# Attention by pairs of heads: full-float32 scores on two row tiles, blocks of 128 queries, and a list-scheduled instruction order

## The chip, the cores and the metric

The kernel runs on one NeuronCore of one Trainium2 chip. The metric is the device time of one execution in microseconds (us), the median of three runs. Times inside an execution come from the hardware profiler and count from its first instruction.

## The reference

Causal attention over 24 heads (2 batches of 12, 448 positions, head size 64) feeds a gated layer and then a mixture of eight experts with one expert per token. Only the attention part is touched by the change.

```python
batch, n_heads, seq, head_dim = (2, 12, 448, 64)

scores = scale * np.matmul(q, k.transpose(0, 1, 3, 2))
scores = np.where(mask, -1000000000.0, scores)          # mask: upper triangle, k=1
scores = scores - np.max(scores, axis=-1, keepdims=True)
attn = np.exp(scores)
attn = attn / (np.sum(attn, axis=-1, keepdims=True) + 1e-09)
return np.matmul(attn, v).astype(np.float32)
...
x = attn_out.transpose(0, 2, 1, 3).reshape(B * S, H * D)     # 896 x 768
gate = 1 / (1 + np.exp(-(x @ w_gate)));  x = gate * (x @ w_val) @ w_out
out = gate_w[:, None] * (np.maximum(x @ w1[e], 0) @ w2[e])   # e: the token's expert
```

## The kernel before

Everything runs in one program whose instruction order on each engine is the order in which the Python code issues it; no engine reorders its own queue. PE does the matmuls, DVE the row maxima and part of the evictions, ACT the exponentials and the other evictions, POOL the normalisation, and the SP queue starts the loads.

**Attention.** Heads go in 24 steps `t`, two to a pair `p`. Queries are cut into four blocks of 112, so that block `c` needs 112(c+1) keys. Per head:

- `at_qk` (L194 for the first head of a pair, L190 and L191 for the second) makes the scores `sc`. The first head is taken as float32 from 64 partitions; the second is split into high and low parts (`at_hi` on DVE, L172; `at_lo` on POOL, L178 and L179), and is two passes over 128 partitions. `sc` lies in four PSUM banks "A".
- `at_max` (L202, DVE) adds the mask, writes the rows to `pr` and takes the row maximum; `at_exp` (L208, ACT) takes the exponential and the row sum; `at_recip` (L213, L214, DVE) and `at_norm` (L220, POOL, four blocks) normalise.
- `at_T` (L232) transposes the ten 112 x 112 blocks of `pr` into two banks "B" (`tp`); `at_ev` (L242 on ACT, L244 on DVE) copies them to `pt`.
- `at_av` (L252) multiplies by `v`, both heads of a pair in the two column halves of one bank `av`; `at_xh` (ACT) and `at_xl` (DVE) split the result into `xh` and `xl`, the operands of the next stage.

**What sets the order.** Two strings of operation names, `ORDER`, one for even and one for odd `t`, written by hand. A head's scores, its maxima, its normalisation, its transposes and its `av` are issued in different steps (`t`, `t-1`, `t-2`, `t-4`, and `(t-6)//2` for the pair).

**Weights.** The gate and value weights arrive as 64-bit numbers in pieces of 128 x 768 (`raw_gv`, through SP). `conv64` turns a piece into float32 in five DVE steps (L97 to L105), then ACT writes the high part (`whi`, L107) and POOL the low part (`wlo`, L108). The first three pieces are converted during attention: the name "w" in `ORDER` takes one DVE step, from `t` = 6 on.

```python
V.scalar_tensor_tensor(t, u[:, :, 0], 29, t, ALU.logical_shift_right, ALU.bitwise_or)
v = t.bitcast(F32)
A.copy(hi, v)
G.tensor_tensor(lo, v, hi.bitcast(F32), ALU.subtract)
```

The last two lines are issued together with the fifth DVE step. Each of the three pieces feeds one `gv` unit of batch 0 (18 matmuls, L273), issued between the last heads. After attention comes the loop over all 24 `gv` units, beginning with unit 0 of batch 1; the rest of the program (the output layer, routing, the experts) isn't touched.

Of the kernel before, what the change touches and what calls it, by code (L numbers as in the profile page):

```python
# [24 lines left out]
CP = 112  # L25
# [10 lines left out]
C_MASK = 0  # L36
C_ID = C_MASK + S
# [10 lines left out]
def _consts():  # L48
    c = np.zeros((128, C_END), np.float32)
    p = np.arange(128)[:, None]  # L50
    c[:, C_MASK + S - CP:C_MASK + S] = np.where(np.arange(CP)[None, :] > p, NEG, 0.0)
# [10 lines left out]
    return c  # L62


def body(tc, i, out):
    nc = tc.nc
    PE, V, A, G, SP = nc.tensor, nc.vector, nc.scalar, nc.gpsimd, nc.sync
    with ExitStack() as ctx:
# [10 lines left out]
        mask = con[:CP, C_MASK:C_MASK + S]  # L79
        ident = con[:, C_ID:C_ID + 128]  # L80

        # x^T, high and low parts, one tile per batch
# [65 lines left out]
        at = ExitStack()  # L148
        ap = at.enter_context(tc.tile_pool(name="attn", bufs=1))
        qk_raw, qk_sp, v_sb = {}, {}, {}  # L150

        # the first head of a pair is taken as float32, the second one is split in high and low parts
        def at_load(p):
            if p >= NH // 2:
                return
            r1 = ap.tile([D, 2, S], F32, tag="raw1", name=f"raw1_{p}", bufs=2)
            SP.dma_start(r1, i["qk0"][p])
            if p == 0:
                SP.dma_start(con[:, :C_IOTA], i["con"][:, :C_IOTA])
            r0 = ap.tile([128, 2, S], F32, tag="raw0", name=f"raw0_{p}", bufs=2)  # L160
            SP.dma_start(r0, i["qk1"][p])
            qk_raw[p] = r0, r1
            v = ap.tile([CP, 2, NCH, D], F32, tag="v", name=f"v{p}", bufs=6)
            SP.dma_start(v, i["v"][p])
            v_sb[p] = v

        def at_hi(p, w):
            if p >= NH // 2:
                return
            if w == 0:  # L170
                qk_sp[p] = [ap.tile([128, S], F32R, tag=n, name=f"{n}{p}", bufs=2) for n in ("qs", "kh", "kl")]
            V.tensor_copy(qk_sp[p][w], qk_raw[p][0][:, w])  # L172

        def at_lo(p):
            if p < NH // 2:
                qs, kh, kl = qk_sp[p]
                r0 = qk_raw[p][0]
                G.tensor_tensor(qs[64:128], r0[64:128, 0], qs[64:128].bitcast(F32), ALU.subtract)  # L178
                G.tensor_tensor(kl, r0[:, 1], kh.bitcast(F32), ALU.subtract)  # L179

        sc_ps, pr, st_, pt_sb, av_ps, tp_ps = {}, {}, {}, {}, {}, {}

        def at_qk(t, c):
            p, h = t // 2, t % 2
            w = CP * (c + 1)
            b = bank("A", f"sc{t}_{c}", 4)
            if h == 1:
                qs, kh, kl = qk_sp[p]
                q = qs[:, c * CP:(c + 1) * CP]
                PE.matmul(b[:CP, :w], q, kh[:, :w], start=True, stop=False)  # L190
                PE.matmul(b[:CP, :w], q, kl[:, :w], start=False, stop=True)  # L191
            else:
                r1 = qk_raw[p][1]
                PE.matmul(b[:CP, :w], r1[:, 0, c * CP:(c + 1) * CP], r1[:, 1, :w], start=True, stop=True)  # L194
            sc_ps[t, c] = b

        def at_max(t, c):
            if c == 0:
                pr[t] = ap.tile([CP, NCH, S], F32, tag="pr", name=f"pr{t}", bufs=5)
                st_[t] = ap.tile([CP, 4 * NCH], F32, tag="st", name=f"st{t}", bufs=5)  # L200
            w = CP * (c + 1)
            V.tensor_tensor_reduce(pr[t][:, c, :w], sc_ps.pop((t, c))[:CP, :w], mask[:, S - w:], -0.125, 3.0e38,  # L202
                                   ALU.add, ALU.min, st_[t][:, c:c + 1])

        def at_exp(t, c):
            w = CP * (c + 1)
            p, s = pr[t], st_[t]
            A.activation(p[:, c, :w], p[:, c, :w], AF.Exp, bias=s[:, c:c + 1], scale=-1.0,  # L208
                         accum_out=s[:, NCH + c:NCH + c + 1])

        def at_recip(t):
            s = st_[t]
            V.tensor_scalar(s[:, 2 * NCH:3 * NCH], s[:, NCH:2 * NCH], 1e-9, None, ALU.add)  # L213
            V.reciprocal(s[:, 3 * NCH:], s[:, 2 * NCH:3 * NCH])  # L214

        def at_norm(t):
            for c in range(NCH):
                w = CP * (c + 1)
                r = st_[t][:, 3 * NCH + c:3 * NCH + c + 1]
                G.tensor_scalar(pr[t][:, c, :w], pr[t][:, c, :w], r, 1.0, ALU.mult, ALU.mult)  # L220

        PT_OFF = [0, 448, 896, 784]

        def at_T(t, g):
            b = bank("B", f"tp{t}_{g}", 2)
            if g == 0:
                pt_sb[t] = ap.tile([CP, 1120], F32, tag="pt", name=f"pt{t}", bufs=4)
            js = [[0], [1, 3], [2]][g]
            off = 0
            for j in js:  # L230
                for c in range(j, NCH):
                    PE.transpose(b[:CP, off:off + CP], pr[t][:, c, j * CP:(j + 1) * CP], ident[:CP, :CP])  # L232
                    off += CP
            tp_ps[t, g] = b

        def at_ev(t, g):
            b = tp_ps.pop((t, g))
            js = [[0], [1, 3], [2]][g]
            o = PT_OFF[js[0]]
            off = CP * sum(NCH - j for j in js)  # L240
            if g == 2 or (g < 2 and t % 2 == 1):
                A.copy(pt_sb[t][:, o:o + off], b[:CP, :off])  # L242
            else:
                V.tensor_copy(pt_sb[t][:, o:o + off], b[:CP, :off])  # L244

        def at_av(p, j):
            if j == 0:
                av_ps[p] = bank(f"C{p % 2}", f"av{p}", 1)
            o = PT_OFF[j]
            n = S - CP * j  # L250
            for h in range(2):
                PE.matmul(av_ps[p][h * 64:(h + 1) * 64, CP * j:S], v_sb[p][:, h, j, :], pt_sb[2 * p + h][:, o:o + n],  # L252
                          start=(j == 0), stop=(j == NCH - 1))
# [9 lines left out]
        gv_ps = {}  # L263

        def gv_mm(u, b):
            hi, lo = gv_w[u]
            acc = bank("A", f"gv{u}_{b}", 4)
            gv_ps[u, b] = acc
            n = 0
            for k in range(KD):  # L270
                wh, wl = hi[:, k * 128:(k + 1) * 128], lo[:, k * 128:(k + 1) * 128]
                for w, x in ((wh, xh[b]), (wh, xl[b]), (wl, xh[b])):
                    PE.matmul(acc[:, :S], w, x[:, k], start=(n == 0), stop=(n == 3 * KD - 1))  # L273
                    n += 1
# [13 lines left out]

        # emission: attention, software pipelined over heads
        at_load(0)  # L290
        at_load(1)
        SP.dma_start(con[:, C_IOTA:], i["con"][:, C_IOTA:])
        at_load(2)
        w_load()
        w_load()
        at_hi(0, 0)
        at_hi(0, 1)
        at_lo(0)

        def first_weights():  # L300
            for u in range(3):
                yield from w_steps("gv", u)

        fw = first_weights()
# [4 lines left out]
        for t in range(NH + 6):  # L309
            ts, tn, tT = t - 1, t - 2, t - 4  # L310
            pa = (t - 6) // 2
            sm, nm, tr, av = 0 <= ts < NH, 0 <= tn < NH, 0 <= tT < NH, 0 <= pa < NH // 2
            for op in ORDER[t % 2]:
                k = int(op[1]) if op[1:].isdigit() else None
                if op == "L":
                    at_load(t // 2 + 3)
                elif op in ("hq", "hk"):
                    at_hi(t // 2 + 1, int(op == "hk"))
                elif op == "lo":
                    at_lo(t // 2) if t else None  # L320
                elif op[0] == "m":
# [21 lines left out]
            if NH <= t < NH + 3:  # L343
                gv_mm(t - NH, 0)
# [504 lines left out]
```

## Time and profile before

| what | us |
|---|---|
| median of three runs (560.64, 562.09, 566.18) | 562.09 |
| span of the profiled execution, first to last instruction | 554.8 |
| attention: first score matmul, to the first matmul of `gv` unit 0 of batch 1 | 4.18 to 124.70 |
| PE busy, share of the span | 95% |
| DVE, ACT, POOL busy, share of the span | 72%, 40%, 33% |

The profiled execution's own time isn't listed beside its span; the span is 7.3 us below the median of the timed runs. Busy shares are averages over stages with different limits, so what attention costs is read from its own stretch.

### The profile page before, as it was taken

Reading aid. Unit: us, or ns where it says so; the run is one execution under the profiler, and the core shown is the slowest. Engines: PE = TensorE matmul, PEld = TensorE weight load, DVE = VectorE, ACT = ScalarE, POOL = GpSimd, SP = SyncE. Lnnn points to the kernel's source line nnn. Section 1 sums busy time; section 2 is a strip of 40 time slices with the busy share of each in tenths; the row PEclk is TensorE's granted clock in tenths of the full one; section 3 lists DMA queues with packets and bytes.
Section 4 is the critical chain, followed back from the end, with each engine's and each line's share of the span. In section 5 each row is a group of like instructions: output and inputs, shape, how many; then the busy total and the mean of one; then the engine's idle time right before and its main releaser. Section 6 shows DMA issues by size and latency. Waiting matters only on the chain.

```text
span 554.8 us, 8622 instructions
## 1 busy us (share of the span) xinstructions
PE 529.4 (95%) x3056; PEld 460.2 (83%) x3056; DVE 399.7 (72%) x785; ACT 223.6 (40%) x497; POOL 185.0 (33%) x191
## 2 busy tenths in 40 slices
PE   5999898999999999989999979899999999999995
PEld 3665555679999899979799869798899999999995
DVE  3899999418888888988875999505358876657650
ACT  3778777613222222221231132322445544535530
POOL 3899999501222222222220445420320110300102
PEclk9999999999999999997999989999999999999999
DMA  8842552001333333333330445111765766865821
GB/s 215 273 133 84 173 167 82 2 0 61 115 115 115 114 114 110 114 107 127 113 115 17 154 147 184 37 33 54 235 180 171 227 219 202 272 193 171 257 83 50
DMA packets 26255, 73.97 MB, mean 133 GB/s; under 512 B 3208, under 2 KB 8590, under 8 KB 26208
## 3 DMA queue, kind: packets, MB, share of 16 engines
q1 hardware_dynamic: 18912, 65.07, 36.9%
q0 software_dynamic: 1328, 5.51, 3.0%
q10 hardware_dynamic: 5968, 2.79, 1.8%
q8 instruction: 26, 0.43, 0.3%
q14 instruction: 21, 0.17, 0.1%
HBM read 68.25 MB, written 5.90 MB: 134 GB/s over the span
## 4 chain that ended last, share of the span: by engine, by line
PE 49%; DVE 27%; issue 12%; DMA 4%; POOL 3%; ACT 3%; SPq 0%; POOLq 0%; ACTq 0%; DVEq 0%
PE gv L273 10%; PE l L611 10%; PE l L623 9%; PE wo L417 5%; PE av L252 4%; PE tp L232 4%; PE sc L194 3%; DVE cvt_gv L103 3%; DVE cvt_gv L101 3%; DVE hl L287 3%; DVE cvt_wo L101 2%; DVE cvt_gv L105 2%; DVE cvt_wo L103 2%; DVE cvt_gv L99 2%; DVE cvt_gv L97 2%
## 5 line engine op out<-in xcount | busy, mean ns | idle before, releaser
L273 PE MATMUL gv<-xh,whi_gv 128*128 128x448 f32 x288 | 106.8, 371 | 2.2 <-ACT sg L283 2.2
L273 PE MATMUL gv<-xh,wlo_gv 128*128 128x448 f32 x288 | 106.8, 371 | 2.1 <-POOL wlo_gv L108 2.1
L273 PE MATMUL gv<-xl,whi_gv 128*128 128x448 f32 x288 | 106.2, 369 | 0.0
L108 POOL TENSOR_TENSOR wlo_gv<-cvt_gv,whi_gv 128x768 fp32r<-128x768 f32 x24 | 44.4, 1848 | 130.4 <-ACT whi_gv L107 123.5
L417 PE MATMUL wo<-hh,wo 128*128 128x448 f32 x288 | 86.4, 373 | 0.0
L623 PE MATMUL l<-w,mh 128*128 128x384 f32 x256 | 65.4, 336 | 0.0
L273 PEld LDWEIGHTS gv<-xh,wlo_gv 128*128 128x128 f32 x288 | 54.9, 191 | 7.7 <-POOL wlo_gv L108 3.3
L273 PEld LDWEIGHTS gv<-xh,whi_gv 128*128 128x128 f32 x288 | 55.0, 191 | 7.4 <-ACT sg L283 2.9
L220 POOL TENSOR_SCALAR pr<-pr,st 112x112 f32<-112x112 f32 (+1 forms) x96 | 56.5, 604 | 8.1 <-DVE st L214 4.9
L273 PEld LDWEIGHTS gv<-xl,whi_gv 128*128 128x128 f32 x288 | 54.8, 190 | 4.3
L417 PEld LDWEIGHTS wo<-hh,wo 128*128 128x128 f32 x288 | 54.5, 189 | 4.6
L208 ACT ACTIVATE pr<-pr,st 112x448 f32<-112x448 f32 (+2 forms) x96 | 49.9, 523 | 14.7 <-DVE st L202 14.7
L611 PE MATMUL l<-xTh,whi_m 128*128 128x256 f32 x192 | 55.3, 288 | 0.0
L611 PE MATMUL l<-xTl,whi_m 128*128 128x256 f32 x192 | 54.3, 283 | 0.0
L611 PE MATMUL l<-xTh,wlo_m 128*128 128x256 f32 x192 | 54.2, 283 | 0.0
L107 ACT CAST whi_gv<-cvt_gv 128x768 fp32r<-128x768 f32 x24 | 20.1, 836 | 84.6 <-DVE cvt_gv L105 84.6
L417 PE MATMUL wo<-hl,wo 128*128 128x448 f32 x144 | 52.9, 368 | 0.0
L623 PEld LDWEIGHTS l<-w,mh 128*128 128x128 f32 x256 | 44.7, 188 | 0.0
L623 PE MATMUL l<-w,ml 128*128 128x384 f32 x128 | 43.1, 336 | 0.0
L585 DVE TENSOR_TENSOR w<-mr,w 128x768 fp32r<-128x768 f32 x32 | 31.2, 977 | 15.9 <-ACT w L584 15.1
L232 PEld LDWEIGHTS tp<-con,pr 112*112 112x112 f32 x240 | 24.4, 136 | 21.1 <-issue 6.8
L287 DVE TENSOR_TENSOR hl<-sg,hh 128x448 fp32r<-128x448 f32 x24 | 29.1, 1211 | 17.8 <-ACT hh L286 17.8
(143 smaller groups left out, 1015.0 us busy)
## 6 DMA issues: line engine op xcount, KB each, us to landing
mr<-in_w SPq DMA_DIRECT2D x64, 384.0 KB, 3.7
raw_gv<-in_wgv SPq DMA_DIRECT2D x24, 768.0 KB, 4.4
raw_wo<-in_wo SPq DMA_DIRECT2D x12, 768.0 KB, 4.3
raw<-in_qk SPq DMA_DIRECT2D x12, 448.0 KB, 5.7
raw<-in_qk SPq DMA_DIRECT2D x12, 224.0 KB, 3.2
v<-in_v SPq DMA_DIRECT2D x12, 224.0 KB, 5.1
x2d<-rows ACTq DMA_DIRECT2D x12, 224.0 KB, 4.1
con<-in_con SPq DMA_DIRECT2D x1, 288.0 KB
```

The lines of the kernel that those rows point to most:

```text
L101: V.tensor_scalar(t, t, 3, 0x3FFFFFF8, ALU.logical_shift_left, ALU.bitwise_and)
L103: V.scalar_tensor_tensor(t, u[:, :, 1], 0xC0000000, t, ALU.bitwise_and, ALU.bitwise_or)
L108: G.tensor_tensor(lo, v, hi.bitcast(F32), ALU.subtract)
L208: A.activation(p[:, c, :w], p[:, c, :w], AF.Exp, bias=s[:, c:c + 1], scale=-1.0, accum_out=s[:, NCH + c:NCH + c + 1])
L220: G.tensor_scalar(pr[t][:, c, :w], pr[t][:, c, :w], r, 1.0, ALU.mult, ALU.mult)
L232: PE.transpose(b[:CP, off:off + CP], pr[t][:, c, j * CP:(j + 1) * CP], ident[:CP, :CP])
L273: PE.matmul(acc[:, :S], w, x[:, k], start=(n == 0), stop=(n == 3 * KD - 1))
L287: V.tensor_tensor(hl[b][:, m], sg[b], hh[b][:, m].bitcast(F32), ALU.subtract)
L417: PE.matmul(acc[:, :S], w, x[:, ft], start=(ft == 0 and z == 0), stop=(ft == KF - 1 and z == 2))
L585: V.tensor_tensor(lo, raw, hi.bitcast(F32), ALU.subtract)
L611: PE.matmul(t[:, :NS], a, x[:, k], start=(z == 0), stop=(z == 3 * KD - 1))
L623: PE.matmul(acc[s][n][:, :384], a, x, start=(f == 0 and z == 0), stop=(f == KF2 - 1 and z == 2))
```

## The change

- Scores of both heads of a pair are taken as float32. For query blocks 0 to 2, now of 128 queries, the first head sits in partitions 0 to 63 and the second in 64 to 127, and each makes its own matmul (L227). The last 64 queries of both heads make one block of 128 rows over 128 partitions (L221), with zeros packed into the host array `qk` where a head's queries meet the other head's keys. The split into high and low parts (L172, L178, L179) is gone.
- A pair has seven blocks ("segments") where it had eight: widths 128, 128, 256, 256, 384, 384 and 448. Maxima, exponentials and normalisation run by segment. The addition of 1e-9 moves from DVE to POOL (`at_eps`), on seven columns at once, so a pair needs one of these and one reciprocal where it needed two of each.
- A pair has 16 transposes of 128 x 128, four to a bank, and four evictions of 512 columns, each on ACT or DVE as the scheduler decides. `at_av` makes 11 matmuls on a pair, 1024 columns for each head.
- Buffers are named by hand: `pr` for four pairs, `pt` for three, `qk` for three, `v` for five.
- The order of all engines until the end of attention comes from `Line`: each operation has a rank, one or more engines with a duration, and the operations it comes after; the earliest possible one is issued next, the lower rank first within 0.1 us. The conversion steps are in it with rank 2000 and up, 0.7 us each on DVE and no time on ACT or POOL; they don't come after the load of their piece.

```diff
+class Line:
+    HOP = {"PE": 0.2, "DVE": 0.12, "ACT": 0.15, "POOL": 0.12, "SP": 2.0}
...
+    def emit(self):
...
+                for e, dur in engines.items():
+                    at = free.get(e, 0.0)
+                    for a in after:
+                        at = max(at, end[a][0] + (0.03 if end[a][1] == e else self.HOP[end[a][1]]))
+                    if m != mode.get(e, m):
+                        at += 0.12
+                    key = (round(at / 0.1), rank, at + dur)
+                    if best is None or key < best[0]:
+                        best = key, n, e, at, dur, m
...
+        def at_qk(p, c):
+            t = qk[p % NQK]
+            if c == 3:
+                b = sc_ps[p, 6] = bank("A", f"sc{p}_6", 4)
+                PE.matmul(b[:, :S], t[:, 384:512], t[:, 512:960], start=True, stop=True)
                 return
...
+            w = QB * (c + 1)
+            for h in range(2):
+                b = sc_ps[p, 2 * c + h] = bank("A", f"sc{p}_{2 * c + h}", 4)
+                r = slice(64 * h, 64 * h + 64)
+                PE.matmul(b[:, :w], t[r, QB * c:QB * (c + 1)], t[r, 512:512 + w], start=True, stop=True)
...
+        def at_eps(p):
+            s = stt[p % NPR]
+            G.tensor_scalar(s[:, 14:21], s[:, 7:14], 1e-9, 1.0, ALU.add, ALU.mult)
...
+        AV = [[((0, 0, 448),), ((512, 0, 384), (448, 384, 64))],
+              [((1024, 128, 320),), ((1408, 128, 256), (1344, 384, 64))],
+              [((1664, 256, 192),), ((1920, 256, 128), (1856, 384, 64))],
+              [((896, 384, 64),), ((960, 384, 64),)]]
...
-        ORDER = (
-            "lo m0 e0 m2 T0 A0 L m1 T1 m3 V0 Q2 Q0 e2 xh e3 Q1 Q3 A1 e1 r T2 n V2 V1 w".split(),
-            "T0 V0 A2 T1 m0 Q2 m1 m2 V1 Q1 Q0 m3 A3 r T2 e3 V2 n e0 xl e1 e2 hq Q3 w hk".split(),
-        )
...
+        for p in range(NP):
+            r = 100 * p
...
+            es = ln.add(r + 30, {"POOL": 0.57}, lambda e, p=p: at_eps(p), [ex[p, g] for g in range(7)])
+            rc = ln.add(r + 31, {"DVE": 0.18}, lambda e, p=p: at_recip(p), [es])
+            for g in (0, 2, 4, 6, 1, 3, 5):
+                nm[p, g] = ln.add(r + 32, {"POOL": 0.6}, lambda e, p=p, g=g: at_norm(p, g), [rc])
...
+        for u in range(3):
+            steps = w_steps("gv", u)
+            for k in range(5):
+                fn = (lambda e, s=steps: next(s, None))
+                last = ln.add(2000 + 10 * u + k, {"DVE": 0.7}, fn, [last])
+            gv = [last, lastq]
+            for k in range(KD):
+                gv = [ln.add(3000 + 10 * u + k, {"PE": 0.61}, lambda e, u=u, k=k: gv_part(u, 0, k),
+                             gv + [mx[7 * NP - 4 + u]] + [xld[p] for p in range(KD)], mode="f")]
```

What stands in a row at three places follows. First DVE at the start of the program, before (`qs` and `kh` are the split of the first pair's second head, each L202 a row maximum):

```order
L172 CAST qs_101<-raw_0_80 128x448
L172 CAST kh_102<-raw_0_80 128x448
L202 ISA pr_122,st_123<-sc_0_116,con 112x112
L202 ISA st_123 112x1
L202 ISA pr_122,st_123<-sc_1_118,con 112x224
```

And DVE at the start now (`mk` is the mask, L139 the first step of a conversion, each L235 a row maximum):

```order
L329 MEMSET mk 128x256
L330 MEMSET mk 128x384
L139 TENSOR_SCALAR cvt_gv_124<-raw_gv_114 128x768
L235 ISA pr_86,st_93<-sc_0_118,mk 128x128
L235 ISA st_93 128x1
L235 ISA pr_86,st_93<-sc_1_120,mk 128x128
```

The first step of the first conversion has moved ahead of the first maximum; before, it stood behind the maxima of six heads.

Second POOL at the low part of the first piece, before (L220 normalises a block, L178 and L179 split the next pair):

```order
L220 TENSOR_SCALAR pr_496<-pr_496,st_497 112x336
L220 TENSOR_SCALAR pr_496<-pr_496,st_497 112x448
L108 TENSOR_TENSOR wlo_gv_368<-cvt_gv_369,whi_gv_367 128x768
L220 TENSOR_SCALAR pr_540<-pr_540,st_541 112x112
L220 TENSOR_SCALAR pr_540<-pr_540,st_541 112x224
```

And now (`pr_88` is the third pair, counted as 2; L244 adds 1e-9, L251 normalises a segment):

```order
L244 TENSOR_SCALAR st_95<-st_95 128x7
L251 TENSOR_SCALAR pr_88<-pr_88,st_95 128x128
L251 TENSOR_SCALAR pr_88<-pr_88,st_95 128x256
L150 TENSOR_TENSOR wlo_gv_123<-cvt_gv_124,whi_gv_122 128x768
L251 TENSOR_SCALAR pr_88<-pr_88,st_95 128x384
L251 TENSOR_SCALAR pr_88<-pr_88,st_95 128x448
```

The low part stood between two heads, and stands now in the middle of a pair's normalisation, ahead of two of the four segments that the pair's first transposes read.

Third PE over most of a pair in the middle of attention, before (scores of two heads, transposes and `av` in turn):

```order
L232 MATMUL tp_1_449<-con,pr_275 112x112 x4
L194 MATMUL sc_2_456<-raw_4_156 112x336
L194 MATMUL sc_0_458<-raw_4_156 112x112
L194 MATMUL sc_1_463<-raw_4_156 112x224
L194 MATMUL sc_3_465<-raw_4_156 112x448
L252 MATMUL av_439<-pt_321,v_88 64x336
L252 MATMUL av_439<-pt_372,v_88 64x336
L232 MATMUL tp_2_472<-con,pr_275 112x112 x2
L232 MATMUL tp_0_482<-con,pr_315 112x112 x4
```

And now, in the second half of attention (the pair whose scores these are is the eleventh; the `av` behind them is one block of eleven matmuls):

```order
L261 MATMUL tp_0_833<-con,pr_86 128x128 x4
L227 MATMUL sc_0_840<-qk_79 128x128
L227 MATMUL sc_1_842<-qk_79 128x128
L227 MATMUL sc_2_846<-qk_79 128x256
L227 MATMUL sc_3_848<-qk_79 128x256
L261 MATMUL tp_1_851<-con,pr_86 128x128 x4
L261 MATMUL tp_2_858<-con,pr_86 128x128 x4
L227 MATMUL sc_4_866<-qk_79 128x384
L227 MATMUL sc_5_868<-qk_79 128x384
L261 MATMUL tp_3_872<-con,pr_86 128x128 x4
L221 MATMUL sc_6_881<-qk_79 128x448
L285 MATMUL av_888<-pt_92,v_84 64x448
```

The four interleaved pieces of `av` have become one block, and the scores come in three groups per pair.

## Rows read from the trace of the kernel before

**Rows 1.** Chain of waits, one pair of heads: start us, us, what

```profile
35.00 2.07 PE sc L194 x8
37.08 0.72 PE av L252 x4
37.79 0.72 PE tp L232 x6
38.51 0.53 PE av L252 x4
39.04 0.53 PE tp L232 x4
40.23 0.34 PE av L252 x4
40.57 0.34 PE tp L232 x2
...
41.31 0.39 PE tp L232 x4
41.70 0.90 PE av L252 x4
42.60 0.53 PE tp L232 x4
43.13 2.07 PE sc L194 x8
...
110.42 3.66 PE gv L273 x18
```

**Rows 2.** Timeline of PE: start us, us, engine line op tiles shapes xcount

```profile
12.68 4.07 PE L194 MATMUL sc<-raw 64*112 64x336 f32 x8
...
18.87 1.46 PE L232 MATMUL tp<-con,pr 112*112 112x112 f32 x8
20.26 2.14 PE L194 MATMUL sc<-raw 64*112 64x336 f32 x8
```

**Rows 3.** Timeline of PE at the end of attention, same columns

```profile
124.70 0.47 PE L273 MATMUL gv<-xh,whi_gv 128*128 128x448 f32 x1
```

**Rows 4.** DMA view, 0 to 40 us: GB/s in slices of 1 us; issues, us to landing

```profile
GB/s 0 0 212 275 223 336 242 231 228 290 287 234 222 222 307 299 381 430 412 246 215 242 242 82 265 297 337 0 0 0 197 255 372 102 0 0 0 8 108 326
...
raw_gv<-in_wgv SPq DMA_DIRECT2D x2, 768.0 KB, 6.9
```

**Rows 5.** Timeline of SP: issue of the first two weight pieces

```profile
11.46 0.90 SPq L91 DMA_DIRECT2D raw_gv<-in_wgv  x2
```

**Rows 6.** Timeline of DVE: the first maximum

```profile
8.29 0.27 DVE L202 CUSTOM_DVE_ANT_0 pr<-sc,con 112x112 f32<-112x112 f32 x1
```

**Rows 7.** Groups by line, 0 to 125 us: xcount, busy us, mean ns, idle before

```profile
L220 POOL TENSOR_SCALAR pr<-pr,st 112x112 f32<-112x112 f32 (+1 forms) x96 | 56.5, 604 | 8.1 <-DVE st L214 4.9 <-PE tp L232 2.8 <-ACT pt L242 0.4
...
L242 ACT COPY pt<-tp 112x224 f32<-112x224 f32 (+1 forms) x48 | 20.7, 438 | 28.9 <-PE tp L232 27.5
...
L213 DVE TENSOR_SCALAR st<-st 112x4 f32<-112x4 f32 x24 | 14.7, 612 | 1.7 <-ACT pr L208 1.6
...
L108 POOL TENSOR_TENSOR wlo_gv<-cvt_gv,whi_gv 128x768 fp32r<-128x768 f32 x3 | 5.5, 1828 | 0.0
...
L105 DVE SCALAR_TENSOR_TENSOR cvt_gv<-raw_gv,cvt_gv 128x768 uint32<-128x768 uint32 x3 | 4.1, 1362 | 0.0
...
L103 DVE SCALAR_TENSOR_TENSOR cvt_gv<-raw_gv,cvt_gv 128x768 uint32<-128x768 uint32 x3 | 2.9, 952 | 0.0
L107 ACT CAST whi_gv<-cvt_gv 128x768 fp32r<-128x768 f32 x3 | 2.5, 836 | 0.5 <-DVE cvt_gv L105 0.5
```

**Rows 8.** A later stretch: length, busy us (xcount) of PE, PEld, DVE, ACT, POOL; granted clock

```profile
248.60:255.50 6.90, 6.12 (x17) 5.45 (x17) 6.73 (x7) 0.83 (x1) 2.56 (x2) 0.51 0.56 201
```

**Rows 9.** Timeline of PE ahead of that stretch; in brackets its idle time

```profile
247.93 0.47 PE L273 MATMUL gv<-xh,whi_gv 128*128 128x448 f32 x1 [1.65 <-ACT sg L283]
...
249.38 0.74 PE L273 MATMUL gv<-xh,wlo_gv 128*128 128x448 f32 x1 [0.78 <-POOL wlo_gv L108]
```

More of the change, by code (lines that the diff above doesn't have):

```diff
@@ L62, in _consts, with _tri, __init__, add @@
     return c
+def _tri():
+    p = np.arange(128)[:, None]
+    t64 = np.where(np.arange(64)[None, :] > p % 64, NEG, 0.0)
+    t128 = np.where(np.arange(128)[None, :] > p, NEG, 0.0)
+    return np.concatenate([t64, t128], axis=1).astype(np.float32)
+class Line:
+    HOP = {"PE": 0.2, "DVE": 0.12, "ACT": 0.15, "POOL": 0.12, "SP": 2.0}
+    def __init__(self):
+        self.ops = []
+    def add(self, rank, engines, fn, after=(), mode=None):
+        self.ops.append((rank, engines, fn, [a for a in after if a is not None], mode))
+        return len(self.ops) - 1
+    def emit(self):
+        free, mode, end = {}, {}, {}
+        left = set(range(len(self.ops)))
+        while left:
+            best = None
+            for n in left:
+                rank, engines, _, after, m = self.ops[n]
+                if any(a not in end for a in after):
+                    continue
+                for e, dur in engines.items():
[7 more added lines that the diff above has]
+                        best = key, n, e, at, dur, m
+            _, n, e, at, dur, m = best
+            left.remove(n)
+            free[e] = at + dur
+            mode[e] = m
+            end[n] = at + dur, e
+            self.ops[n][2](e)
 def body(tc, i, out):
@@ L167, in at_hi @@
[L167 to L179, printed above, removed]
@@ L197, in at_max @@
[L197 to L209, printed above, removed]
@@ L211, in at_recip @@
[L211 to L253, printed above, removed]
+        NP, QB = NH // 2, 128
@@ new lines, in body, with mask_c @@
+        NPR, NPT, NQK, NV = 4, 3, 3, 5
+        SEG = [(0, 128), (768, 128), (128, 256), (896, 256), (384, 384), (1152, 384), (1536, S)]
+        SEG_END = 1536 + 512
+        mk = ap.tile([128, 832], F32, tag="mk", name="mk")
+        mask_s = mk[:, 0:S]
+        def mask_c(c):
+            return mk[:, 832 - QB * (c + 1):832]
+        qk = [ap.tile([128, 960], F32, tag=f"qk{n}", name=f"qk_{n}") for n in range(NQK)]
+        vt = [ap.tile([128, 2, 4, D], F32, tag=f"v{n}", name=f"v_{n}") for n in range(NV)]
@@ new lines, in at_av @@
+        def at_av(p):
+            b = av_ps[p] = bank(f"C{p % 2}", f"av{p}", 1)
+            t = ptt[p % NPT]
+            for j in range(4):
+                for n in range(2):
+                    for h in range(2):
+                        if n < len(AV[j][h]):
+                            o, q, w = AV[j][h][n]
+                            PE.matmul(b[64 * h:64 * h + 64, q:q + w], vt[p % NV][:, h, j, :], t[:, o:o + w],
+                                      start=(j == 0 and n == 0), stop=(j == 3), skip_group_check=True)
@@ L263, in body, with gv_part @@
         gv_ps = {}
+        def gv_part(u, b, k):
+            hi, lo = gv_w[u]
+            if k == 0:
+                gv_ps[u, b] = bank("A", f"gv{u}_{b}", 4)
+            acc = gv_ps[u, b]
+            wh, wl = hi[:, k * 128:(k + 1) * 128], lo[:, k * 128:(k + 1) * 128]
+            for z, (w, x) in enumerate(((wh, xh[b]), (wh, xl[b]), (wl, xh[b]))):
+                PE.matmul(acc[:, :S], w, x[:, k], start=(k == 0 and z == 0), stop=(k == KD - 1 and z == 2))
         def gv_mm(u, b):
[L266 to L269, printed above, removed]
             for k in range(KD):
[L271 to L274, printed above, removed]
+                gv_part(u, b, k)
         sg = {}
@@ L292, in body @@
+        at_loadv(0)
+        at_load(2)
+        at_loadv(1)
         SP.dma_start(con[:, C_IOTA:], i["con"][:, C_IOTA:])
-        at_load(2)
+        at_loadv(2)
         w_load()
         w_load()
[L296 to L304, printed above, removed]
-        ORDER = (
-            "lo m0 e0 m2 T0 A0 L m1 T1 m3 V0 Q2 Q0 e2 xh e3 Q1 Q3 A1 e1 r T2 n V2 V1 w".split(),
-            "T0 V0 A2 T1 m0 Q2 m1 m2 V1 Q1 Q0 m3 A3 r T2 e3 V2 n e0 xl e1 e2 hq Q3 w hk".split(),
-        )
@@ L347, in body @@
+        ln.emit()
         at.close()
```

173 lines of the change are left out of this document (99 added, 74 removed).

## The prediction

> **What bounds the kernel now.** I read the chain of waits first, over the attention stretch alone. From 27 to 57 us it is PE on PE: one pair of heads after another, 8.13 us from one `sc` row to the same row of the next pair (35.00 to 43.13), with hardly an entry of another engine [rows 1]. So there a microsecond of PE work per pair is a microsecond of span. The reader should see two more things in these rows. Four transposes take 0.39 us behind the second head's scores and 0.53 us behind `av` or the first head's scores: 0.14 us is the price of a change between the three shapes in which the array is used (full, 64 rows, 64 columns), and a pair has nine changes. And `av` over 448 columns takes 0.90 us for both heads; less the change that is (0.90 - 0.14) / 448 = 1.70 ns a column for two heads together, whereas the first head's scores, 1120 columns on 64 rows, take (2.07 - 0.14) / 1120 = 1.72 ns a column for one. Two column tiles thus run beside each other at nearly the price of one.
>
> Then the timeline of PE. At the start it runs at half pace: eight matmuls of a first head take 4.07 us at 12.68 and 2.14 us at 20.26 [rows 2]. The first transposes start at 18.87, and the first matmul of the next stage at 124.70 [rows 3]; the stage behind it runs from PE too, so I carry a shift of this point to the end one to one. The stretch from 18.87 to 124.70 is 105.8 us.
>
> **A pair on PE after the change.** Scores: blocks of 128, 256 and 384 columns on two row tiles, 768 columns, then 448 columns on the full array. No row of before shows two row tiles at once. The bounds are beside each other, 768 x 1.72 = 1.32 us, and one behind the other, 2.64 us. I take the first, because the column tiles are the nearest row and each row tile has a bank of its own. The last block is 448 x 1.72 = 0.77 us. Transposes: 16 of 128 columns at 0.39 / 448 = 0.87 ns a column make 1.78 us (before 0.72 + 0.53 + 0.34 + 0.39 + 0.53 = 2.51). `av`: 1024 columns a head, 1.74 us (before 2.49 with its changes). That is 5.61 us; the order of the later pairs has six changes, 0.84 us; together 6.45 against 8.13.
>
> The Trainium skill ("TensorE: Matmul & The Clock Gate", section "Measured speedup vs the span model") gives 3.07 times for four row tiles, not four times. No run here shows it; by that share, 77%, the 1.32 us would be 1.72.
>
> **The other engines** have room at this pace. POOL loses both splits and has seven segments in place of eight blocks, 7 x 0.60 us, and one short addition of at most 0.6: 4.8 of 6.45 us. DVE loses the splitting copies and the additions of 1e-9, short instructions that last 612 ns on the mean, 14.7 us in all [rows 7]. ACT has one exponential less a pair, and fewer columns. I cost these at nothing as long as PE is the bound; where a chain through them is late, it is counted below.
>
> **The start.** This I cost as a loss. The first conversion step now stands ahead of the first maximum on DVE, and it needs the first weight piece. Behind it are queued all maxima, so all exponentials, and PE stops when its four banks are full. Before, the piece was issued at 11.46 and landed 6.9 us later, at 18.4 [rows 4, 5], behind three pairs of loads and the constants: 4016 KB with itself. The first bytes move at 2.0 us, so 245 KB a us. Now 3408 KB go with it or ahead of it (three `qk` of 480 KB, three `v` of 256, masks 96, constants 336, the piece 768), so it lands at 2.0 + 13.9 = 15.9, and the first maximum comes at 16.5 in place of 8.29 [rows 6]. From the first maximum to the first transposes it was 10.6 us before, at half pace; the same chain, now with six maxima of the second pair ahead of the reciprocal but nothing to split, I take as 10: transposes from 26.5, 7.6 us later. If the piece lands as late as before, it is 2.5 more; a faster queue might save 1.5.
>
> **From there on.** PE's work from the first transposes to the end, by the prices above: twelve pairs of transposes and `av` 12 x 3.52 = 42.2; scores of nine pairs and one last block 9 x 2.09 + 0.77 = 19.6; three `gv` units of 3.66 us, 11.0; and 60 changes counted along the order of after, 8.4. That is 81.2 us, and 107.7 for the end if PE never waits.
>
> It will wait at three places. The list gives a conversion step 0.7 us and knows nothing of the high and low part issued with the fifth. POOL is in order, so the segments behind a low part wait for the fifth step, the high part and the low part, and PE's transposes wait for the segments. At the third piece, counted from the end of the maxima ahead of it, the chain is 0.95 + 1.36 + 0.84 + 1.83 + two segments at 0.60 = 6.2 us [rows 7], and PE has an `av` less half a microsecond, scores, four transposes and four changes in hand, 3.6 us: a wait of 2.6. By the same walk it is 2.7 at the first piece and 2.3 at the second: 7.6 us. The bounds are zero, if POOL is that far ahead, and three times the 4.0 us that POOL stands on account of one piece.
>
> At the end, all eight evictions of the last two pairs are on ACT: 0.44 us at 336 columns on the mean [rows 7], near 0.6 at 512, against 0.45 for the four transposes, with two banks, and the last `av` waits for the last one. I add 2 us.
>
> Waits of this size can cost clock too: later in the program 1.65 and 0.78 us of PE's idle time within 3.1 us were followed by a fall [rows 9] of the granted clock to 0.51, that is 1.2 GHz, for 6.9 us, in which 17 matmuls took 6.12 us [rows 8], 2.7 us more than at the 0.203 us each of the `gv` rows in attention. I count one such fall; the bounds are none and three.
>
> **The sum.** 26.5 + 81.2 + 7.6 + 2 + 2.7 = 120.0, against 124.70: 4.7 us less. The profiled span, 554.8, would be 550.1. The median of the runs, 562.09, lies 7.3 us above the span; with that kept, 557.4 us. What the pairs gain, some 20 us in twelve, is mostly given back at the start and behind the low parts.
>
> **Rivals.**
> - *The waits are covered.* POOL has 1.6 us a pair to spare and the list issues transposes a pair later than the scores, so segments may be ready early. Then neither the waits nor the fall of the clock come: 120.0 - 10.3 = 109.7, 547.1 us. Against it stands the order itself: the low part is in the middle of a pair whose transposes are next. If half of it is covered, 552.
> - *The row tiles run one behind the other.* Then a pair costs 1.32 us more, over nine pairs 11.9 us, and the time is 569.3, slower by 1.3%. It decides from some 1.1 us a pair on. For it: no row shows row tiles together. Against it: the column tiles.
> - *The row tiles overlap in part.* If two of them together take 1.3 times one, where the column tiles take (0.90 - 0.14) / (448 x 1.72 ns) = 0.99 times one, a pair costs 0.40 us more, nine pairs 3.6 us: 561.0, no change. Nothing in the rows speaks for a part. The Trainium skill's page "TensorE: Matmul & The Clock Gate", section "Measured speedup vs the span model", does, with its 3.07 of four.
> - *The start is longer and the clock falls three times.* 2.5 + 5.4 us: 565.3, still within 1%; with an order that is late by half a microsecond a pair at other places too (a hand-written order stood there, without such waits), 571.
>
> **How the numbers follow.** About 1% (5.6 us) is what a measurement of this kernel can tell from no change. The forecast, a small gain within that, gets 0.32; the overlap in part 0.05 and a longer start 0.06, both within 1% too: 0.43. Covered waits, wholly or by half, get 0.36, all faster by over 1%. Row tiles in sequence get 0.12 and the late order 0.09: 0.21 slower. The range reaches from the covered waits, 547, to the row tiles in sequence, 570; the likeliest case alone, with the bounds of start and clock, is 553 to 565.
>
> **What the profile would show.** Right: the first L235 starts near 16.5 us, right behind the first L139; score matmuls of a pair's two heads start together, and a pair late in attention takes 6.4 to 6.6 us; before three `tp` groups PE is idle 2 to 3 us, released by POOL; the first `gv` matmul of batch 1 is near 120. Wrong: a first maximum near 9, or no idle time with POOL as releaser (then the gain is larger); or pairs of 7.5 us or more late in attention (then it is the tiles). What would make the prediction wrong outside these is a change in the later stages, which run the same instructions.

## The result

The changed kernel takes 553.61 us at the median (550.61 to 555.34, four runs), the kernel before 561.6 us in the runs beside it (560.64 to 566.18, four). The ratio is 0.9849 with an interval of 0.98 to 0.9898: 1.5% faster, with the whole interval below 0.99. The forecast was 557.4 us, 4.7 us less than before; 8.0 us less were measured. The time lies in the range, but the gain is past the 1% within which the likeliest case was put. Ratios here and below are estimated without the slow executions that this program sometimes has, so they differ a little from the quotients of the medians.

The profiled execution of after took 555.34 us, and its span is 553.6 us. The time is 1.7 us above the span of the same execution, and in the other kernels run here it was 1.7 to 1.9 us too.

**The start.** DVE's timeline of after, at the start; columns as in [rows 6]:

```profile
12.31 0.56 DVE L139 TENSOR_SCALAR cvt_gv<-raw_gv 128x768 uint32<-128x768 uint32 x1 [10.78 <-DMA raw_gv<-in_wgv]
12.79 0.28 DVE L235 CUSTOM_DVE_ANT_0 pr<-sc,mk 128x128 f32<-128x128 f32 x1
```

DVE does nothing for 10.78 us but wait for the first weight piece, and the first maximum follows the conversion step at once: 12.79 us, against 8.29 before [rows 6]. The order of events is the one forecast, and the load is 3.6 us earlier. The issue of the piece in SP's timeline of after, and then the DMA view of after from 0 to 40 us (GB/s in slices of 1 us), follow:

```profile
6.64 0.90 SPq L133 DMA_DIRECT2D raw_gv<-in_wgv  x2
```

```profile
GB/s 0 0 184 294 273 377 412 416 401 421 449 424 406 221 0 0 0 54 265 369 66 31 200 382 150 123 342 27 8 0 16 72 191 104 338 425 396 15 0 0
```

SP issues the pieces 4.8 us earlier than before [rows 5]. Before, the third pair's loads stood ahead of them and had to wait for the first pair's two `raw` buffers, 3.0 us until PE had made its scores and 1.8 us until POOL had made its split; `qk` now has a buffer for each of the first three pairs. SP's timeline of before at these two loads:

```profile
8.29 0.47 SPq L157 DMA_DIRECT2D raw<-in_qk  x1
10.60 0.33 SPq L161 DMA_DIRECT2D raw<-in_qk  x1
```

And from 6 to 13 us the loads of after run at 401 to 449 GB/s, where the same seven slices of before show 222 to 290 [rows 4]. The 3408 KB that I counted took (12.3 - 2.0) = 10.3 us, 331 KB a us and not 245.

**PE from there on.** PE's timeline of after: the first transposes, every wait behind them up to the end of attention, and the first `gv` matmul of batch 1:

```profile
13.14 1.86 PE L227 MATMUL sc<-qk 64*128 64x384 f32 x4 [6.14 <-DVE st L235]
...
22.86 0.77 PE L261 MATMUL tp<-con,pr 128*128 128x128 f32 x4
...
33.68 0.41 PE L261 MATMUL tp<-con,pr 128*128 128x128 f32 x2 [0.61 <-ACT pt L267]
35.56 0.33 PE L261 MATMUL tp<-con,pr 128*128 128x128 f32 x1 [1.47 <-POOL pr L251]
36.18 0.33 PE L261 MATMUL tp<-con,pr 128*128 128x128 f32 x1 [0.29 <-POOL pr L251]
...
55.91 0.44 PE L261 MATMUL tp<-con,pr 128*128 128x128 f32 x2 [1.75 <-POOL pr L251]
...
73.29 0.33 PE L261 MATMUL tp<-con,pr 128*128 128x128 f32 x1 [1.64 <-POOL pr L251]
73.86 1.15 PE L261 MATMUL tp<-con,pr 128*128 128x128 f32 x6 [0.23 <-POOL pr L251]
...
111.44 1.15 PE L261 MATMUL tp<-con,pr 128*128 128x128 f32 x8 [0.24 <-ACT pt L267]
112.86 1.17 PE L261 MATMUL tp<-con,pr 128*128 128x128 f32 x8 [0.28 <-ACT pt L267]
...
118.84 0.47 PE L305 MATMUL gv<-xh,whi_gv 128*128 128x448 f32 x1
```

There are three waits of transposes for POOL's normalisation, 2.37, 1.75 and 1.87 us with what stands right beside them, 6.0 in all (0.61 of the first is a wait for an eviction on ACT), and at the end 0.52 us for evictions on ACT. POOL's timeline of after at the first one:

```profile
30.41 2.12 POOL L251 TENSOR_SCALAR pr<-pr,st 128x128 f32<-128x128 f32 x2 [1.19 <-DVE st L248]
33.13 1.81 POOL L150 TENSOR_TENSOR wlo_gv<-cvt_gv,whi_gv 128x768 fp32r<-128x768 f32 x1 [0.60 <-ACT whi_gv L149]
34.92 2.57 POOL L251 TENSOR_SCALAR pr<-pr,st 128x384 f32<-128x384 f32 x5
```

Two segments are done, then POOL stands 0.60 us for the high part, spends 1.81 on the low part, and only then does the third segment, for which PE waits at 35.56. That is the walk of the prediction.

**The clock.** Windows of after behind the first and the third wait (columns as in [rows 8]; behind the second, from 57.2 us, it reads the same), and the stretch of 13.9 us around the first:

```profile
36.80:40.20 3.40, 3.40 (x16) 1.52 (x14) 2.73 (x11) 0.44 (x3) 0.90 (x3) 0.50 0.06 25
...
74.30:77.70 3.40, 3.40 (x14) 2.14 (x12) 1.54 (x5) 3.31 (x12) 1.76 (x4) 0.50 0.13 25
```

```profile
27.70:41.60 13.90, 11.53 (x83) 7.31 (x82) 8.95 (x27) 8.38 (x26) 9.31 (x15) 0.88 0.34 113
```

Behind each of the three waits the granted clock stands at 0.50 or 0.51, that is 1.2 GHz, for 3.4 us: at half pace 1.7 us lost each time, 5.1 in all. I had counted one fall.

**The pair.** The chain of waits of after, one late pair from `av` to `av`; columns as in [rows 1]:

```profile
83.96 1.91 PE av L285 x16
85.87 0.59 PE tp L261 x4
86.46 0.86 PE sc L227 x8
87.31 1.02 PE tp L261 x8
88.34 0.85 PE sc L227 x4
89.18 0.58 PE tp L261 x4
89.77 0.76 PE sc L221 x2
90.52 1.91 PE av L285 x16
```

Without a wait a pair takes 90.52 - 83.96 = 6.56 us, against 8.13 before [rows 1]. Six of these seven pieces begin with a change between shapes (0.14 us each; `sc` L221 follows `tp` in the same shape). The scores of blocks 0 to 2 are then 0.86 + 0.85 - 0.28 = 1.43 us, transposes 2.19 - 0.42 = 1.77, `av` 1.77, the last block 0.76.

### The profile page after: what moved, and what is told of

Same layout as the page of the kernel before. It is cut to its first block, busy times and chain, and to the rows that moved or that the text cites. A ratio compares the mean times of both kernels' runs of the same rounds, so it can differ in the third digit from the quotient of the medians.

```text
span 553.6 us, 8346 instructions
## 1 busy us (share of the span) xinstructions
PE 517.5 (93%) x3056; PEld 454.6 (82%) x3056; DVE 369.8 (67%) x698; ACT 214.9 (39%) x454; POOL 147.2 (27%) x171
## 3 DMA queue, kind: packets, MB, share of 16 engines
q10 hardware_dynamic: 6192, 3.07, 2.0%
## 4 chain that ended last, share of the span: by engine, by line
PE 47%; DVE 27%; issue 12%; POOL 4%; ACT 4%; DMA 4%; SPq 1%; POOLq 0%; ACTq 0%
PE l L666 10%; PE l L678 9%; PE gv L305 8%; PE wo L472 5%; PE tp L261 4%; DVE cvt_gv L143 4%; PE sc L227 4%; DVE cvt_gv L145 3%; PE av L285 3%; DVE cvt_wo L143 3%; DVE hl L322 3%; DVE cvt_wo L145 2%; DVE cvt_gv L147 2%; PE sc L221 2%; DVE cvt_gv L141 2%
## 5 line engine op out<-in xcount | busy, mean ns | idle before, releaser
L240 ACT ACTIVATE pr<-pr,st 128x128 f32<-128x128 f32 (+3 forms) x84 | 43.9, 526 | 12.0 <-DVE st L235 11.8
L251 POOL TENSOR_SCALAR pr<-pr,st 128x128 f32<-128x128 f32 (+3 forms) x84 | 43.2, 536 | 16.1 <-DVE st L248 16.1
L322 DVE TENSOR_TENSOR hl<-sg,hh 128x448 fp32r<-128x448 f32 x24 | 29.1, 1211 | 17.8 <-ACT hh L321 17.8
L227 PE MATMUL sc<-qk 64*128 64x128 f32 (+2 forms) x144 | 28.0, 477 | 10.7 <-DVE st L235 6.1
```

The lines of the kernel that those rows point to most:

```text
L227: PE.matmul(b[:, :w], t[r, QB * c:QB * (c + 1)], t[r, 512:512 + w], start=True, stop=True)
L240: A.activation(seg(p, g), seg(p, g), AF.Exp, bias=s[:, g:g + 1], scale=-1.0, accum_out=s[:, 7 + g:8 + g])
L251: G.tensor_scalar(seg(p, g), seg(p, g), stt[p % NPR][:, 21 + g:22 + g], 1.0, ALU.mult, ALU.mult)
L322: V.tensor_tensor(hl[b][:, m], sg[b], hh[b][:, m].bitcast(F32), ALU.subtract)
```

## The experiments

All are edits of the changed kernel, and their times are compared with the kernel before in the same rounds (median 562.75 us for the first four, 563.25 for the next three, 564.15 for the last). In those where the order is edited, the list scheduler no longer calls an operation when it places it but collects the order, and the edited order is then issued; line numbers shift by a few.

**Are the falls of the clock a matter of PE's idle time?** Ahead of the transposes that wait, PE gets three, two and two matmuls that nobody reads:

```diff
+            for _ in range({(2, 0): 3, (4, 1): 2, (6, 1): 2}.get((p, q), 0)):
+                PE.matmul(b[:, :448], ident, con[:, :448], start=True, stop=True)
```

> Seven needless matmuls of 448 columns (float32, constants) stand on PE ahead of the three groups of transposes that wait for POOL; results are not touched. If the three falls of the granted clock to 0.5 (36.8, 57.2 and 74.3 us in the trace of the changed kernel) come from these idle times, they go away though the waits stay: 3 x 3.41 us at half pace give back 1.7 us each, so the first gv matmul of batch 1 comes at 113.5 to 114.5 instead of 118.84, and the time is about 5 us lower than the changed kernel's, near 548.5. If the falls are set by something else, clock and time stay (553 to 555).

Measured: 547.94 us (546.03 to 550.08), ratio 0.9761 (0.9709 to 0.9813). PE's timeline of this kernel at the first place and at the end of attention, and its window over the first place:

```profile
33.42 2.52 PE L260 MATMUL tp<-con 128*128 128x448 f32 x6 [0.52 <-ACT pt L269]
...
113.62 0.47 PE L307 MATMUL gv<-xh,whi_gv 128*128 128x448 f32 x1
```

```profile
27.70:41.60 13.90, 13.38 (x100) 9.02 (x98) 10.03 (x30) 9.86 (x31) 10.10 (x17) 1.00 0.38 130
```

The segments come no earlier, PE only works in place of waiting, and the clock stays at 1.00, in this stretch and in those of the other two places. The next stage begins 118.84 - 113.62 = 5.2 us earlier, which is the 5.1 us of the falls and 0.2 of an earlier first transpose (22.64). The six timed executions bear this out: their mean granted clock over the whole program is 0.985 to 0.992, that of the four of after 0.980 to 0.983. Useless work at the right place gains 5 us; the intervals of the two ratios still touch (0.9709 to 0.9813, and 0.98 to 0.9898), so that it is the trace that shows the gain.

**Are the waits made by the place of the low part?** The low part of each piece is taken out of the fifth conversion step and issued on POOL behind the seventh segment of the pair in whose middle it stood:

```diff
         A.copy(hi, v)
+        yield
         G.tensor_tensor(lo, v, hi.bitcast(F32), ALU.subtract)
...
+        extra = {max((nm[p, g] for g in range(7)), key=at_): u for u, p in enumerate((2, 4, 6))}
+        for n, e in seq:
+            ln.ops[n][2](e)
+            if n in extra:
+                next(cv[extra[n]][5], None)
```

> Only the three low parts are moved on POOL, each from the middle of a pair's normalisation to its end; all else stands in the same order. My theory (POOL stands for the high part, and PE's transposes for POOL): the waits of 2.4, 1.75 and 1.9 us on PE go, and with them the three falls of the clock, 1.7 us each: 11 us, first gv matmul of batch 1 at 108 to 109, time 542 to 544. Rival (DVE or ACT is as late as POOL, and the wait only changes its name): idle time before the same transposes stays over 1 us each, and the time is within 3 us of 553.6.

Measured: 544.33 us (541.97 to 545.96), ratio 0.9693 (0.9641 to 0.9744). The two longest of the three waits of PE that are left from the first transposes (23.85) to 97 us, and the start of the next stage:

```profile
34.56 0.63 PE L263 MATMUL tp<-con,pr 128*128 128x128 f32 x4 [0.61 <-ACT pt L269]
...
66.26 0.66 PE L263 MATMUL tp<-con,pr 128*128 128x128 f32 x4 [0.46 <-ACT pt L269]
...
109.17 0.47 PE L307 MATMUL gv<-xh,whi_gv 128*128 128x448 f32 x1
```

No transpose waits for POOL any more, and no fall of the clock is left in attention (1.00 in three stretches over the same places). Of the 9.7 us at the first `gv` matmul, 4.8 are waits (6.0 less 1.2 that remain) and 5.1 falls, and a start 1.0 us later takes 1.0 back: 8.9, so 0.8 us stay without a term. The prediction's rival "the waits are covered" gave 109.7 us for this point.

**What does the first conversion step cost at its place?** It is moved to just ahead of the second, behind the first maxima; the low parts stay:

```diff
+        one = seq.pop(at_(cv[0][0]))
+        seq.insert(at_(cv[0][1]), one)
```

> Only the first conversion step is moved on DVE, from ahead of the first maximum to just ahead of the second conversion step. My theory: the first maximum comes when scores and mask are there, at 6 us instead of 12.8, the first transposes near 16, and the 7 us stay to the end: first gv matmul of batch 1 at 112 to 113, time near 547. Rival (the loads of the second and third pair or the half clock set the pace of the start anyway, or the first wait for POOL takes the gain back): less than half of it, 550 to 553.

Measured: 544.67 us (542.95 to 547.78), ratio 0.9712 (0.9659 to 0.9765). DVE's timeline of this kernel at the first maximum, then PE's at the first transposes, at the waits and at the next stage, and the windows of its two falls:

```profile
5.63 0.29 DVE L236 CUSTOM_DVE_ANT_0 pr<-sc,mk 128x128 f32<-128x128 f32 x1 [4.10 <-DMA mk<-in_tri]
```

```profile
15.08 0.82 PE L262 MATMUL tp<-con,pr 128*128 128x128 f32 x4
...
28.58 0.33 PE L262 MATMUL tp<-con,pr 128*128 128x128 f32 x1 [1.47 <-POOL pr L252]
...
48.91 0.44 PE L262 MATMUL tp<-con,pr 128*128 128x128 f32 x2 [1.76 <-POOL pr L252]
64.67 2.10 PE L262 MATMUL tp<-con,pr 128*128 128x128 f32 x7 [1.63 <-POOL pr L252]
...
109.71 0.47 PE L306 MATMUL gv<-xh,whi_gv 128*128 128x448 f32 x1
```

```profile
30.50:33.90 3.40, 3.40 (x18) 1.94 (x18) 2.09 (x10) 0.00 (x0) 1.37 (x5) 0.50 0.00 0
64.60:68.00 3.40, 3.25 (x9) 2.09 (x10) 1.19 (x4) 1.99 (x8) 1.08 (x4) 0.50 0.31 124
```

The first maximum waits for the mask alone and comes 7.2 us earlier, the first transposes 7.8, the next stage 9.1. The three waits are as long as in after; behind the second, of 1.76 us, the clock didn't fall in this execution, which is about the rest of the gain (1.3 us, for 1.7 a fall). This execution is the fastest of the six, with the highest mean clock (0.985, the others 0.976 to 0.982), so the fall may well have come in the others.

**Do the two add up?** Both moves in one kernel.

> Both moves of the two kernels ahead of this one together. If both theories hold and the parts add up, 7 + 11 us less than the changed kernel: first gv matmul of batch 1 at 101 to 103, time 535 to 538. If the start's gain is taken back at the first wait, that wait is gone here, so it would show here alone: 7 us below the run with the low parts moved.

Measured: 536.47 us (533.83 to 538.37), ratio 0.955 (0.9499 to 0.9601). The next stage begins at 101.00 us, 17.8 earlier than in after, where the moves alone gave 9.7 and 9.1, 18.8 together; one fall of 1.7 us is counted in both of these. The start and the low parts are two separate costs, and without both of them attention ends 23.7 us before the 124.70 of before [rows 3].

**Do the row tiles run beside each other?** Here the scores of blocks 0 to 2 are taken on the full array: each head's queries stand over 128 partitions, with zeros where they meet the other head's keys, so that the result is the same. The loads of `qk` grow from 960 to 1344 columns.

```diff
-                r = slice(64 * h, 64 * h + 64)
-                PE.matmul(b[:, :w], t[r, QB * c:QB * (c + 1)], t[r, 512:512 + w], start=True, stop=True)
+                o = 384 * h + QB * c
+                PE.matmul(b[:, :w], t[:, o:o + QB], t[:, 896:896 + w], start=True, stop=True)
```

> The changed kernel, but the blocks of 128 queries make their scores on the full array: each head's queries are packed with zeros in the other head's partitions, so both heads' matmuls run one after the other over 128 rows, and the change of array shape around the scores is gone. If the row tiles overlap as I costed them, a pair pays 768 columns more, 1.3 us, and saves four changes of 0.14: 0.7 us more a pair, 6 us over nine pairs, less what the waits for POOL cover, and 1.7 us for loads that are 576 KB longer at the start: 557 to 561. If the row tiles ran one behind the other in the changed kernel, nothing is lost and the changes are saved: 548 to 550.

Measured: 554.81 us (553.04 to 557.27), ratio 0.9872 (0.9819 to 0.9925): no difference from after (0.98 to 0.9898). Neither of the two expected times, so the profile has to say why. The chain of waits over one late pair, PE's waits on POOL, and the window over the first of them:

```profile
85.60 1.91 PE av L285 x16
...
90.29 1.29 PE sc L227 x4
...
92.77 1.91 PE av L285 x16
```

```profile
39.36 0.33 PE L261 MATMUL tp<-con,pr 128*128 128x128 f32 x1 [1.47 <-POOL pr L251]
...
59.41 0.44 PE L261 MATMUL tp<-con,pr 128*128 128x128 f32 x2 [1.64 <-POOL pr L251]
75.81 0.33 PE L261 MATMUL tp<-con,pr 128*128 128x128 f32 x1 [0.62 <-POOL pr L251]
...
121.45 0.47 PE L305 MATMUL gv<-xh,whi_gv 128*128 128x448 f32 x1
```

```profile
27.70:41.60 13.90, 11.56 (x79) 8.71 (x78) 10.20 (x35) 10.44 (x31) 10.89 (x19) 1.00 0.55 183
```

The pair answers the question. Two heads of 384 columns take 1.29 us one behind the other, and 0.85 - 0.14 = 0.71 us on the row tiles of after; the pair takes 7.17 us, 0.61 more, even though it pays two changes of shape in place of six. The tiles run beside each other: together they take 0.71 / 0.645 = 1.10 times what one head takes.

But the clock doesn't fall. PE is idle here as long as in after at the first place (11.56 us busy of 13.90, there 11.53), and for 1.47 us at a stretch in both, and the granted clock is 1.00 where after has 0.88. Over the whole program, five of the six timed executions have a mean clock of 0.989 to 0.996; the sixth has 0.975, so falls came there, in attention or later. In the profiled one the balance at the next stage, 121.45 against 118.84, is: first transposes 3.8 us later (26.62), nine pairs 5.5 us more, waits 1.2 less, falls 5.1 less, 3.0 together, with 2.6 measured. What the tiles gain, the falls of the clock take away.

**Can the list do it by itself?** The start and the parts are told to the list, with no edit of the order: the first step comes after the third pair's last maximum, the steps have the lengths of their rows, and the high and low part are operations of ACT and POOL.

```diff
-        last = None
+        last = mx[7 * 2 + 6]
...
-                last = ln.add(2000 + 10 * u + k, {"DVE": 0.7}, fn, [last])
+                last = ln.add(2000 + 10 * u + k, {"DVE": (0.7, 0.7, 0.8, 0.95, 1.36)[k]}, fn, [last])
+            last = ln.add(2000 + 10 * u + 5, {"ACT": 0.84}, fn, [last])
+            last = ln.add(2000 + 10 * u + 6, {"POOL": 1.83}, fn, [last])
```

> The list is told what it didn't know, and nothing is moved by hand: the conversion starts after the third pair's last maximum, each step has its own length, and the high part (ACT 0.84 us) and the low part (POOL 1.83 us) are operations of their own. If the two faults of the order are all there was, it is as fast as the hand-made moves, 534 to 538. Rival: the list puts the low parts at other places where PE waits, 540 or more.

Measured: 533.22 us (531.68 to 536.53), ratio 0.9502 (0.9448 to 0.9556), 4.98% faster than the kernel before. All of PE's waits from 21 to 97 us, and the next stage:

```profile
61.00 0.88 PE L263 MATMUL tp<-con,pr 128*128 128x128 f32 x6 [0.23 <-POOL pr L253]
83.76 1.15 PE L263 MATMUL tp<-con,pr 128*128 128x128 f32 x8 [0.29 <-ACT pt L269]
97.94 0.47 PE L307 MATMUL gv<-xh,whi_gv 128*128 128x448 f32 x1
```

The order of the list is as good as the one moved by hand, and 3.1 us better at this point; the intervals of the two ratios overlap.

**Do the list's other errors cost something?** The same, with all other durations of the list set to those of the trace.

> The same two corrections as in the version with the start and the parts told to the list, and beside them the list's other durations (a change of shape 0.14 us, maxima 0.07 us plus their width, exponentials 0.285 us plus width, evictions 0.5 on ACT and 0.61 on DVE, normalisation 0.52, the two splits of the result 0.43 and 0.52) set to those measured in the trace of the changed kernel. Theory (the list's errors cost time only where a whole operation is missing or an operation comes too early, as the three low parts and the first conversion step did): no gap of PE above 0.3 us stood in attention after the start in that version, so there is nothing left to take: 531 to 536, ratio to before 0.945 to 0.956. Rival (wrong durations cost something at every pair): the first matmul of the next stage comes 2 to 4 us before 97.94 and the time is 529 to 531.

Measured: 534.43 us (532.2 to 535.98), ratio 0.9506 (0.9462 to 0.955), with the next stage at 99.13 us. No difference: with the start and the parts told to it, the list gains nothing by right durations for the rest.

**How steady is the profile of before?** The kernel before, unchanged, profiled once more.

> The kernel before, unchanged, for a second profile and for span beside time of the same executions. The spans of the other runs are 1.8 us below their times, so the first profiled execution of the kernel before, span 554.8, was about 556.6 us, below its median. If that execution was short in attention, the first gv matmul of batch 1 comes later than 124.70 here by the difference; if attention is always the same and the later stages vary, it is at 124.7 within 0.5 and the difference is behind it.

Measured: 562.35 us over ten runs, ratio 1.0031 (0.9989 to 1.0073); the profiled execution took 562.23 us with a span of 560.4. PE's timeline of this execution, where it differs from the one shown of before:

```profile
11.26 0.62 PE L190 MATMUL sc<-kh,qs 128*112 128x336 f32 x1 [2.83 <-POOL qs L178]
...
52.80 0.97 PE L252 MATMUL av<-pt,v 112*64 112x448 f32 x4 [0.98 <-DVE xl L260]
...
127.88 0.47 PE L273 MATMUL gv<-xh,whi_gv 128*128 128x448 f32 x1
```

The first `gv` matmul of batch 1 comes at 127.88 us, not at 124.70 [rows 3]: PE waits 2.83 us for the first split here, 1.16 in the first execution, and 0.98 once more at 52 us. The execution that the prediction was summed on, with a span of 554.8 us, took some 556.6 us if its time stood 1.8 above its span as in the other runs: a short one, below the least of its own timed runs (560.64), though 555.49 and 556.05 us occurred among the later ones.

## Why the prediction was right, and where it was off

The mechanism held: PE bounds attention, a pair is 1.57 us cheaper (changes of shape included, 0.66 in the scores, 0.58 in `av`, 0.32 in the transposes), the first conversion step gives back several us, and the low parts make PE wait at three places and cost clock. Undoing the two costs one by one and together shows them to be what they were said to be. By the prediction's own terms, at the first `gv` matmul of batch 1:

| term | forecast, us | measured, us |
|---|---|---|
| first transposes | 26.5 | 22.86 |
| PE's work from there | 81.2 | 84.4 |
| three waits for POOL | 7.6 | 6.0 |
| end of attention | 2 | 0.5 |
| falls of the clock | 2.7 | 5.1 |
| sum | 120.0 | 118.84 |

(The work is what is left of 118.84 - 22.86 = 95.98 us without the waits, the half microsecond and the falls.)

- *The start.* Right that the first maximum waits for the piece, and the 10 us from there to the first transposes were right too (10.07). The rate was the mis-sized term, 245 KB a us for 331. It came from a start in which SP stood still for 4.8 us ahead of the piece; the third `qk` buffer, which ends this, was there to be seen in the change. The rate that the loads reach now, 401 to 449 GB/s, had no row of before save three slices of 381 to 430 from 16 us on [rows 4]. Why they are faster stays open: from 6 to 13 us packets fill the time of the sixteen DMA engines in both kernels (the profile's share is 1.05 before and 1.04 after, for 248 and 418 GB/s), so that the queue ran short before is not what this view shows.
- *The pair.* 6.56 us against 6.45. Transposes, `av`, the last block and the changes are within 0.03 us of their terms; the scores on the row tiles are 1.43, not 1.32. The rival of tiles in sequence is refuted by the full-array run, and the overlap in part was right in kind, at 1.10 times one tile's time instead of 1.3. The Trainium skill ("TensorE: Matmul & The Clock Gate", section "Measured speedup vs the span model") has 3.07 of four for four row tiles, of 32 rows each; here two float32 tiles give 1.29 / 0.71 = 1.82 of two. Of the 3.2 us by which all of PE's work was off, 1.0 is this, 0.4 is `av` (12 x 0.03), 0.6 the `gv` units (11.6, not 11.0); the rest I haven't split.
- *The waits.* The right places, releaser and mechanism, 6.0 us for 7.6 (5.4 without the wait for ACT); two of the three are below the 2 to 3 us that were named as the sign. The chain is shorter than the walk had it: the last two conversion steps on DVE took 1.03 and 0.99 us on the mean instead of 0.95 and 1.36 [rows 7], and a segment 0.54 instead of 0.60, together 0.4 us at each of three places.
- *The clock.* One fall for three waits was a choice between the bounds "none and three", and three came. That waits lead to falls was right in after; the full-array run shows that it isn't the idle time alone.
- *The end.* The evictions on ACT make PE wait twice, as forecast, for 0.52 us and not 2.
- *The base.* 3.2 us of the difference are in no term. The sum was made on an execution whose attention ended at 124.70; the second one ended at 127.88, with a time close to the median. Against that, attention ends 9.0 us earlier in after. The step that failed is the last one of the sum: the 7.3 us by which the median exceeds the span were kept as if they lay around the span, when 5.5 of them were this execution being short.

The 4.7 us thus became 9.0 at the end of attention: 1.2 by errors in the terms and 3.2 by the base. That the sum came out at 120.0 for 118.84 is luck in good part: its terms were off by -3.6, +3.2, -1.6, -1.5 and +2.4 us. The 8.0 us of the medians lie 1.0 below the 9.0. That a shift is carried to the end one to one was not borne out by single executions: what follows attention, which the change doesn't touch, took 430.1 us in the first profiled execution of before, 434.8 in that of after, and 430.1 to 435.5 in all ten. I haven't traced what varies there.

## What to carry to other kernels

When a list sets the order, look first for what it isn't told: an operation without a duration on an engine that is in order (here 1.8 us on POOL), or without the transfer that it waits for, stands in front of work that could go on, and the price is paid on the bound engine (at the first `gv` matmul, 9.7 us for the low parts with the falls of the clock, 9.1 for the load). Put side by side, the whole change was worth 1.5%, and with these two told to the list 5%. And before a sum is made on one profiled execution, take its own time or profile it twice: this one was some 5.5 us below its median.

## What the runs showed that I had not expected

- **The same wait, with and without a fall of the clock.** In after PE waits 1.47 us and is busy for 11.53 of 13.90 us, and the clock falls to 0.5 for 3.4 us; with scores on the full array, 1.47 us and 11.56 of 13.90, it stays at 1.00. With the first step moved, two of three waits of 1.5 to 1.8 us lead to a fall. So the wait alone doesn't decide. Whether it is what PE does around it, or something that differs from one execution to the next, these runs don't say; one profiled execution of each kernel is little for that.
- **PE's first matmuls run at half pace, and longer with a pause of 6 us among them.** In after, PE works from 4.38 to 7.0 us and waits to 13.14, and its matmuls reach full pace between 16.7 and 19.9. Where the maxima aren't held up, full pace is reached at about 9.8 us. The granted clock doesn't show this half pace: it reads 1.00 from 0 to 19.9 us in after. PE's timeline of the version told to the list, twelve matmuls at full pace (2.14 us; at half pace as many took 3.87 in the version with the first step moved):

```profile
9.87 2.14 PE L229 MATMUL sc<-qk 64*128 64x128 f32 x12
```

Behind a pause of the same kind the version with the needless matmuls is at full pace from 17.6 us on, and the one with the low parts moved only from 21.8, which goes with its later first transposes; why they differ isn't shown.

- **Loads at the start.** 401 to 449 GB/s over seven slices. The Trainium skill ("Perfetto Trace Analysis", section "Roofline") gives about 435 GB/s as the limit of the sixteen DMA engines of one core, and the trace agrees within some 3%: the mean of the seven slices is 418 GB/s, six lie below the limit and one, at 449, a little above.
